# Gate weights of the first columns loaded in quarters, and the table load placed behind the second root

## The chip, the cores and the metric

The kernel runs on one core of a Trainium2 chip. The core has five engines that run side by side, each with its own list of instructions, executed in order: TensorE (PE in the profile; its weight loads are shown as PEld), VectorE (DVE), ScalarE (ACT), GpSimd (POOL) and the sync engine (SP), which issues DMA transfers. The metric is the device time of one execution in microseconds. Eight executions of the kernel before took 178.55 to 178.87 us, with a median of 178.8 us.

## The reference

The input x is a sequence of 2048 rows of 512 values (bf16). Its rows are normalized, and the result goes into two branches whose outputs are added to x:

```python
xn = _layernorm(x, axis=-1)
# A: a global filter in the frequency domain
X = rfft2(xn);  y_A = irfft2(X * (w_r + 1j * w_i), s=(S, D))
# B: a gated feed-forward block
g = einsum("bsd,df->bsf", xn, w_gate)      # 512 -> 1792
u = einsum("bsd,df->bsf", xn, w_up)        # 512 -> 1792
h = gelu_tanh(g) * u
y_B = einsum("bsf,fd->bsd", h, w_down)     # 1792 -> 512
return x + y_A + y_B
```

Layernorm here is `(x - mean) / sqrt(var + 1e-5)`. The change concerns the very beginning of the feed-forward branch: the first rows of x, the first columns of `w_gate` and the first products g and u.

## The kernel before

The 2048 rows are cut into 16 chunks of 128 rows (chunk c holds the rows 16p + c, one per partition p). Per chunk, VectorE takes mean and variance (`bn_stats`, L339, and `bn_aggr`, L342), the reciprocal root of the variance is formed, the rows are normalized to `xn`, and `xn` is transposed to `xnT`, so that the 512 inputs, as four blocks of 128, lie along the partitions. These four blocks (index e) are the contraction blocks of the gate and up products.

The feed-forward branch is a list of units (`todo`, L548 to L551). A unit computes g for some chunks and some blocks of 128 output columns into PSUM, u likewise, then gelu of g on ScalarE (L507) and the product with u on VectorE (L512), which gives a piece of `hT`. The first four units handle one chunk each: units 0 and 1 chunk 0, columns 0 to 511 and 512 to 1023; units 2 and 3 the same for chunk 1. Their sums are split over the contraction: before, each in two halves, blocks 0 and 1, then blocks 2 and 3 (`mm_part`, L502, 8 matmuls of 128x128x128 per half and unit). So TensorE can begin with half of the weights present. The units after these take two or four chunks at a time and come from L494. The down product (L833) and the inverse transform (L837) end the kernel.

The spectral branch runs between these units: folds on VectorE, small matmuls with cosine and sine tables, a twist with the filter weights, and exchanges through DMA.

What sets the order of the work: each engine's instructions are put in order by a planner written out in the kernel (`Plan`). Every operation has an engine, an estimated occupation and latency, its predecessors, a key (the lower, the sooner among those that could start) and possibly an earliest time `t_min`; counted resources stand for buffers (tags "G" and "U" for the sums of g and u, two buffers each; for units 0 to 3, "G" holds g and u of units 0 and 1, "U" those of units 2 and 3). The planner's times decide only the order; on the chip each instruction waits for the semaphores of what it needs.

All loads at the start are issued by the sync engine in program order (L281 to L306): x chunks 0 and 1, an index table, the gate weights of columns 0 to 1023 in two transfers of two contraction blocks (512 KB each), x chunks 2 and 3, the up weights of these columns likewise, x chunks 4 to 7 in two transfers, the remaining columns of both weights (768 KB each), x chunks 8 to 11 in two transfers, then tables, more of x, and the filter weights. The built program has eight completion semaphores for these transfers and uses them in turn: a transfer waits, before it is issued, for the completion of the one eight places before it.

`first_two` (L374) writes out chunks 0 and 1. Their root is `Sqrt` on ScalarE (L394) followed by a reciprocal on VectorE. Chunk 0 is normalized in two halves and transposed by TensorE (L351); chunk 1's transposes (`t`, 0 and 1) stand among the gate matmuls of units 0 and 1, after their first half (`between`, L532, with the keys of L422 and L423). VectorE copies the first half of chunk 1's transposes to `xnT`, ScalarE the second (`copyt1`). `Sqrt` and gelu need different activation tables, so ScalarE has to load the gelu table once after the last `Sqrt`; before, the planner has an entry for it, `table`, which issues no instruction (L412), and the load stands directly in front of the first gelu. TensorE is kept busy by 37 matmuls on zeros from the start (L320), and five more after chunk 0's transposes (L324).

Of the kernel before, what the change touches and what calls it, by code (L numbers as in the profile page):

```python
# [15 lines left out]
AF = mybir.ActivationFunctionType  # L16

S = 2048
# [3 lines left out]
NE = 4  # L22
# [179 lines left out]
def kernel(  # L202
# [80 lines left out]
    idx_t = pc.tile([P, 3], I32, name="idx_t")  # L283
    nc.sync.dma_start(out=idx_t[:], in_=nc.inline_tensor(idx_np, name="spec_rows").ap())  # L284
    for T in (Wg_sb, Wu_sb):
        for e in range(0, NE, 2):
            load_w(T, 0, 1024, e=slice(e, e + 2))
        if T is Wg_sb:
            load_x(2, 2)
    load_x(4, 2)  # L290
    load_x(6, 2)
    load_w(Wg_sb, 1024, DF)
    load_w(Wu_sb, 1024, DF)
    load_x(8, 2)
    load_x(10, 2)
    for c in range(0, NC, 8):
        nc.sync.dma_start(out=RF_t[:, c:c + 8], in_=rf_d.rearrange("p (c k) -> p c k", c=NC)[:, c:c + 8])
    load_x(12, 2)
# [8 lines left out]

    LAND = {0: 2.7, 1: 3.4, 2: 7.2, 3: 7.2}
    LAND.update({c: 11.5 if c < 8 else 17.5 if c < 12 else 20.5 for c in range(4, NC)})
    WG_LAND = [6.6] * 8 + [13.2] * 6  # L310
    WU_LAND = [9.9] * 8 + [15.2] * 6
    RF_LAND = 19.0

# [60 lines left out]
    def first_two():  # L374
        o = {}

        def v(k, fn, occ, deps=(), lat=None, t_min=0.0):
            o[k] = add("DVE", occ, fn, [o[d] for d in deps], key=-2000 + len(o), lat=lat, t_min=t_min,
                       after=o.get("last"))
            o["last"] = o[k]  # L380

        def T(c, h):
            o["T", c, h] = add("PE", 0.12, lambda: f_T(c, 2 * h, 2), [o["xn", c, h]], key=-2000 + 2 * c + h,
                               lat=0.36, acq=("S",))

        def xn_(c, h):
            v(("xn", c, h), lambda: f_norm_v(c, 256 * h, 256), 0.27, [("recip", c)], lat=0.4)

        def stats(c):
            v(("stats", c), lambda: f_stats(c), 0.6, t_min=LAND[c], lat=0.7)  # L390

        def mean(c):
            v(("mean", c), lambda: f_mean(c), 0.17, [("stats", c)])
            o["root", c] = add("ACT", 0.31, lambda: A.activation(  # L394
                out=rstd[:, c:c + 1], in_=mv[:, c, 1:2], func=AF.Sqrt, bias=eps_t[:], scale=1.0),
                [o["mean", c]], key=-2000 + c)

        def recip(c):
            v(("recip", c), lambda: V.reciprocal(out=rstd[:, c:c + 1], in_=rstd[:, c:c + 1]), 0.15, [("root", c)])

        stats(0)
        mean(0)
        stats(1)

        recip(0)
        xn_(0, 0)
        mean(1)
        xn_(0, 1)
        T(0, 0)
        T(0, 1)  # L410
        add("PE", 0.28, spin_on, [o["T", 0, 1]], key=-1500, lat=0.28, after=o["T", 0, 1])
        table = add("ACT", 1.3, lambda: None, [o["root", 1]], key=-1500, lat=1.3)  # L412
        v("copy0", lambda: f_Tc(0, 0, 2), 0.25, [("T", 0, 0)], lat=0.4)
        o["copy0"].rel = ("S",)
        xT_op[0, 0] = o["copy0"]
        recip(1)
        v("copy1", lambda: f_Tc(0, 2, 2), 0.25, [("T", 0, 1)], lat=0.4)
        o["copy1"].rel = ("S",)
        xT_op[0] = o["copy1"]
        xn_op[0] = o["xn", 0, 1]  # L420
        v("xn1", lambda: f_norm_v(1, 0, D), 0.33, [("recip", 1)], lat=0.45)
        o["t", 0] = add("PE", 0.12, lambda: f_T(1, 0, 2), [o["xn1"]], key=1000.13, lat=0.3, acq=("S",))  # L422
        o["t", 1] = add("PE", 0.12, lambda: f_T(1, 2, 2), [o["xn1"]], key=1000.14, lat=0.3, acq=("S",),  # L423
                        after=o["t", 0])
        between.update(o)
        v("copyt0", lambda: f_Tc(1, 0, 2), 0.25, [("t", 0)], lat=0.4)
        o["copyt1"] = add("ACT", 0.4, lambda: f_Tc(1, 2, 2, A.copy), [o["t", 1], table], key=-1400)
        o["copyt0"].rel = o["copyt1"].rel = ("S",)
        xT_op[1, 0] = o["copyt0"]
        xT_op[1] = o["copyt1"]  # L430
        xn_op[1] = o["xn1"]
# [42 lines left out]
    def unit(k, c0, n, f0, m=1):  # L474
# [19 lines left out]
                    T_.matmul(b[name][:, f], lhsT=W_[:, e, (f0 + f) * P:(f0 + f + 1) * P], rhs=rhs[:, e, :],  # L494
                              start=(e == 0), stop=(e == NE - 1))

        def mm_part(name, tag, W_, e0):
            if e0 == 0:
                b[name] = ps.tile([P, m, w], F32, name=name, tag=tag, bufs=2)
            for e in (e0, e0 + 1):  # L500
                for f in range(m):
                    T_.matmul(b[name][:, f], lhsT=W_[:, e, (f0 + f) * P:(f0 + f + 1) * P], rhs=rhs[:, e, :],  # L502
                              start=(e + f == 0), stop=(e == NE - 1), skip_group_check=True)
# [18 lines left out]

        gt, ut = "G", "U"
        if k < 4:
            def parts(name, tag, W_, key, t):
                o = None
                for e in (0, 2):
                    o = add("PE", occ / 2, lambda e=e: mm_part(name, tag, W_, e), [o] if o else [], lat=occ / 2 + 0.3,
                            key=key + 0.1 * e, acq=() if o else (tag,), t_min=t[e // 2])
                    o.deps.append(xT_op[c0, 0] if e == 0 else xT_op[c0])  # L530
                    if k == 1 and W_ is Wg_sb:
                        between["t", 0].deps.append(o) if e == 0 else o.deps.append(between["t", 1])  # L532
                return o

            gt = ut = "GU"[k // 2]
            g = parts("g_ps", gt, Wg_sb, 1000 + 0.1 * (k % 2) + 0.4 * (k // 2), (5.3, WG_LAND[0]))
            u = parts("u_ps", ut, Wu_sb, 1001 + 0.1 * (k % 2) + 0.4 * (k // 2), (8.6, WU_LAND[0]))
        else:
            g = split("g_ps", "G", Wg_sb, 1000 + k, WG_LAND, m)
            u = split("u_ps", "U", Wu_sb, 1000.5 + k, WU_LAND, m)  # L540
# [356 lines left out]
```

## Time and profile before

| | |
|---|---|
| median of 8 executions | 178.8 us (178.55 to 178.87) |
| profiled execution | 178.65 us, of which the span on the core is 177.0 us |
| TensorE busy | 171.7 us, 97% of the span |
| VectorE busy | 115.4 us, 65% |
| ScalarE busy | 96.4 us, 54% |
| GpSimd busy | 16.7 us, 9% |
| DMA | 19.35 MB, mean 109 GB/s; 344 to 390 GB/s from 4.4 to 22 us |
| gate and up sums of the first four units (L502) | 64 + 64 matmuls, from 6.10 to 14.5 us |
| gelu table load | 1.28 us, at 7.82 us |

The span runs from the first to the last instruction on the core; the profiled execution's time is 1.65 us longer than its span. Times in timelines are microseconds from the start of the span. A busy time counts the modelled ends of pipelined matmuls, so a busy TensorE is not one at its peak. The chain of work is followed back from the last instruction, at each step to what released it. In answers on waits a releaser is inferred from semaphores: the last to come is named. In the windows, each engine's entry is its busy time in the window with the number of instructions, then come the clock granted to TensorE, the busy share of the DMA engines, and GB/s.

### The profile page before, as it was taken

The numbers are of one execution on the slowest core, as the hardware profiler recorded it, in microseconds if no ns is written. First come the engines' busy times: TensorE is split into PE (matmuls) and PEld (weight loads), VectorE is DVE, ScalarE is ACT, GpSimd is POOL, SyncE is SP. The second block draws the span as 40 slices with busy tenths as digits, with TensorE's granted clock in tenths as the row PEclk, the third lists the DMA queues.
The fourth block names the chain that finished last, engine by engine and source line by source line (L and its number), as shares of the span: only waits on it lengthen the run. The fifth ranks groups of instructions, "written<-read, shape, count | busy, mean of one in ns | idle before, by whom it ended". The sixth has DMA issues, their size and how long they took to land.

```text
span 177.0 us, 3177 instructions
## 1 busy us (share of the span) xinstructions
PE 171.7 (97%) x1158; PEld 97.1 (55%) x1176; DVE 115.4 (65%) x255; ACT 96.4 (54%) x171; POOL 16.7 (9%) x38
## 2 busy tenths in 40 slices
PE   7999999999999999999999999999999999999993
PEld 7899845455545544555555454555445445444463
DVE  3568999988334499969899799843516325345333
ACT  4362489997734998889999973544112111211200
POOL 1020330407750000000000000000000000000000
DMA  4999999364609602111112312010122222221212
GB/s 100 347 390 381 344 195 150 61 82 94 225 20 313 224 0 59 44 34 44 38 26 61 94 56 59 17 46 0 59 90 89 79 74 66 82 88 60 63 59 59
DMA packets 20848, 19.35 MB, mean 109 GB/s; under 512 B 8481, under 2 KB 17953, under 8 KB 20833
## 3 DMA queue, kind: packets, MB, share of 16 engines
q1 hardware_dynamic: 20416, 17.84, 36.4%
q0 software_dynamic: 416, 1.32, 2.5%
q8 instruction: 9, 0.15, 0.3%
q14 instruction: 7, 0.05, 0.1%
HBM read 13.38 MB, written 2.10 MB: 87 GB/s over the span
## 4 chain that ended last, share of the span: by engine, by line
PE 91%; DMA 4%; SPq 2%; issue 1%; DVE 0%
PE y_ps L833 27%; PE g_ps L494 25%; PE u_ps L494 25%; DMA Wu_sb<-in_B_w_up_dram 4%; PE dp L651 2%; PE yp L784 2%; PE gp L754 2%; PE bp L593 2%; PE y_ps L837 2%; PE ep L660 2%; PE u_ps L502 2%; SPq L277 1%; SPq L273 1%; PE tp L351 0%; SPq L284 0%
## 5 line engine op out<-in xcount | busy, mean ns | idle before, releaser
L494 PE MATMUL g_ps<-xnT,Wg_sb 128*128 128x512 bf16 (+1 forms) x220 | 52.7, 364 | 0.3
L494 PE MATMUL u_ps<-xnT,Wu_sb 128*128 128x512 bf16 (+1 forms) x216 | 52.5, 363 | 0.3
L833 PE MATMUL y_ps<-Wd_sb,hT 128*128 128x512 bf16 (+2 forms) x246 | 50.8, 355 | 0.3
L512 DVE TENSOR_TENSOR hT<-u_ps,ge 128x512 bf16<-128x512 f32 x56 | 38.3, 687 | 17.3 <-PE u_ps L494 12.4
L507 ACT ACTIVATE ge<-g_ps 128x512 bf16<-128x512 f32 x56 | 33.2, 599 | 21.9 <-PE g_ps L494 19.1
L833 PEld LDWEIGHTS <-hT 128*128 128x128 bf16 x252 | 23.2, 98 | 22.2
L494 PEld LDWEIGHTS <-Wg_sb 128*128 128x128 bf16 x224 | 21.5, 98 | 20.9
L494 PEld LDWEIGHTS <-Wu_sb 128*128 128x128 bf16 x224 | 21.4, 98 | 20.2
L790 ACT CAST yf<-yp 128x512 bf16<-128x512 f32 x16 | 9.3, 586 | 39.4 <-PE yp L784 39.4
L840 DVE TENSOR_TENSOR y_sb<-y_ps,y_sb 128x512 bf16<-128x512 f32 (+2 forms) x18 | 11.1, 631 | 27.9 <-PE y_ps L837 27.9
L665 ACT CAST E<-ep 64x512 bf16<-64x512 f32 x32 | 18.5, 579 | 2.0 <-PE ep L660 1.6
L339 DVE BATCH_NORM_STATS2 stats<-x_t 128x6 f32<-128x512 bf16 x16 | 10.3, 672 | 2.7 <-DMA x_t<-in_A_x_dram 2.7
L456 ACT ACTIVATE xn<-x_t,nb,rstd 128x512 bf16<-128x512 bf16 x12 | 9.4, 807 | 0.6 <-POOL nb L370 0.4
L563 ACT CAST Gs<-gp 128x512 bf16<-128x512 f32 x16 | 8.7, 592 | 1.0 <-PE gp L754 1.0
L563 ACT CAST ds<-dp 128x512 bf16<-128x512 f32 x16 | 8.9, 597 | 0.0
L796 DVE TENSOR_TENSOR lv<-yf 128x512 bf16<-128x512 bf16 x16 | 6.1, 420 | 4.1 <-ACT yf L790 3.2
L563 ACT CAST Bs<-bp 128x512 bf16<-128x512 f32 x16 | 8.3, 600 | 0.5 <-PE bp L593 0.5
L784 PEld LDWEIGHTS <-Gs 128*128 128x128 bf16 x64 | 4.8, 98 | 3.5
L803 DVE TENSOR_TENSOR yt<-lv 128x512 bf16<-128x512 bf16 x16 | 6.1, 421 | 0.3
L837 PE MATMUL y_ps<-yt,RI_t 128*128 128x512 bf16 (+2 forms) x18 | 6.1, 355 | 0.0
L784 PE MATMUL yp<-CT,Gs 128*128 128x128 bf16 x64 | 6.0, 219 | 0.1
L697 DVE TENSOR_TENSOR m<-X,TW 128x1024 bf16<-128x1024 bf16 x8 | 5.5, 687 | 0.2
(67 smaller groups left out, 131.6 us busy)
## 6 DMA issues: line engine op xcount, KB each, us to landing
F<-F SPq DMA_DIRECT2D x32, 64.0 KB, 2.0
y_sb<-in_A_x_dram SPq DMA_DIRECT2D x16, 128.0 KB, 2.1
out_dram<-y_sb SPq DMA_DIRECT2D x15, 128.0 KB, 1.7
x_t<-in_A_x_dram SPq DMA_DIRECT2D x7, 256.0 KB, 8.7
Wd_sb<-in_B_w_down_dram SPq DMA_DIRECT2D x1, 1792.0 KB, 7.6
Wg_sb<-in_B_w_gate_dram SPq DMA_DIRECT2D x2, 512.0 KB, 4.3
Wu_sb<-in_B_w_up_dram SPq DMA_DIRECT2D x2, 512.0 KB, 6.8
Wg_sb<-in_B_w_gate_dram SPq DMA_DIRECT2D x1, 768.0 KB, 10.3
```

The lines of the kernel that those rows point to most:

```text
L339: V.bn_stats(out=st[:], in_=x_t[:, c, :])
L456: xn_op[c] = add("ACT", 0.72, lambda c=c: A.activation(out=xn[:, c, :], in_=x_t[:, c, :], func=AF.Identity, bias=nb[:, c:c + 1], scale=rst ...
L494: T_.matmul(b[name][:, f], lhsT=W_[:, e, (f0 + f) * P:(f0 + f + 1) * P], rhs=rhs[:, e, :], start=(e == 0), stop=(e == NE - 1))
L507: A.activation(out=b["ge"][:], in_=b["g_ps"][:], func=AF.Gelu_apprx_tanh)
L512: V.tensor_tensor(out=hT_of(sb, f0, m, o, w), in0=b["u_ps"][:], in1=b["ge"][:], op=ALU.mult)
L563: A.copy(out=o, in_=i)
L665: A.copy(out=b["E"][64 * h:64 * h + 64, r], in_=b["ep", h][64 * r:64 * r + 64])
L784: T_.matmul(t[:, q], lhsT=late["G"][:, q, c0 + j], rhs=IQ[q], start=(q == 0), stop=(q == 3), skip_group_check=True)
L790: A.copy(out=b["yf"][:, j], in_=b[j][:])
L833: T_.matmul(b[o][:], lhsT=hT_of(sb, f, 1, cl * P, P)[:, 0], rhs=Wd_sb[:, f, o:o + w], start=(f == 0), stop=False)
L837: T_.matmul(b[o][:], lhsT=late["RI"][:, c, :], rhs=late["yt"][:, c, o:o + w], start=False, stop=True)
L840: V.tensor_tensor(out=b["y"][:, o:o + w], in0=b[o][:], in1=b["y"][:, o:o + w], op=ALU.add)
```

## The change

Four things are edited.

1. The first 1024 columns of the gate weights come in four transfers of one contraction block (256 KB each) instead of two of two blocks. The up weights stay in two.
2. The gate sums of units 0 to 3 are advanced by quarters, one contraction block at a time (4 matmuls per unit), with keys of their own: blocks 0 and 1 of units 0 and 1, then chunk 1's transposes, then block 2 of units 0 and 1, block 3 of unit 0, blocks 0 and 1 of units 2 and 3, block 3 of unit 1, and blocks 2 and 3 of units 2 and 3. The up sums stay in halves in the same order as before. The number of matmuls is the same.
3. The planner's `table` entry now issues an instruction, a gelu of one column (`warm`), so that the table load stands directly behind the second root and ahead of `copyt1`.
4. x chunks 4 to 7 come in one transfer instead of two, and chunks 8 to 11 too. With edit 1 the number of transfers is as before, but the places of the semaphores shift: the transfers of the up weights are two places later.

Apart from this, every engine's order of instructions is as it was.

```diff
     for T in (Wg_sb, Wu_sb):
-        for e in range(0, NE, 2):
-            load_w(T, 0, 1024, e=slice(e, e + 2))
+        m = 1 if T is Wg_sb else 2
+        for e in range(0, NE, m):
+            load_w(T, 0, 1024, e=slice(e, e + m))
         if T is Wg_sb:
             load_x(2, 2)
-    load_x(4, 2)
-    load_x(6, 2)
+    load_x(4, 4)
     load_w(Wg_sb, 1024, DF)
     load_w(Wu_sb, 1024, DF)
-    load_x(8, 2)
-    load_x(10, 2)
+    load_x(8, 4)
...
-    WG_LAND = [6.6] * 8 + [13.2] * 6
+    WG_LAND = [7.3] * 8 + [13.2] * 6
...
-        table = add("ACT", 1.3, lambda: None, [o["root", 1]], key=-1500, lat=1.3)
+        table = add("ACT", 1.3, lambda: A.activation(out=warm[:], in_=eps_t[:], func=AF.Gelu_apprx_tanh), [o["root", 1]], key=-1500, lat=1.3)
...
-        o["t", 0] = add("PE", 0.12, lambda: f_T(1, 0, 2), [o["xn1"]], key=1000.13, lat=0.3, acq=("S",))
-        o["t", 1] = add("PE", 0.12, lambda: f_T(1, 2, 2), [o["xn1"]], key=1000.14, lat=0.3, acq=("S",),
+        o["t", 0] = add("PE", 0.12, lambda: f_T(1, 0, 2), [o["xn1"]], key=1000.04, lat=0.3, acq=("S",))
+        o["t", 1] = add("PE", 0.12, lambda: f_T(1, 2, 2), [o["xn1"]], key=1000.05, lat=0.3, acq=("S",),
                         after=o["t", 0])
...
-        def mm_part(name, tag, W_, e0):
+        def mm_part(name, tag, W_, e0, ne):
             if e0 == 0:
                 b[name] = ps.tile([P, m, w], F32, name=name, tag=tag, bufs=2)
-            for e in (e0, e0 + 1):
+            for e in range(e0, e0 + ne):
...
-            def parts(name, tag, W_, key, t):
-                o = None
-                for e in (0, 2):
-                    o = add("PE", occ / 2, lambda e=e: mm_part(name, tag, W_, e), [o] if o else [], lat=occ / 2 + 0.3,
-                            key=key + 0.1 * e, acq=() if o else (tag,), t_min=t[e // 2])
-                    o.deps.append(xT_op[c0, 0] if e == 0 else xT_op[c0])
+            def parts(name, tag, W_, keys, t):
+                o, ne = None, NE // len(keys)
+                for i, key in enumerate(keys):
+                    e = i * ne
+                    o = add("PE", occ / len(keys), lambda e=e: mm_part(name, tag, W_, e, ne), [o] if o else [],
+                            lat=occ / len(keys) + 0.3, key=key + 0.01 * (k % 2), acq=() if o else (tag,), t_min=t[i])
+                    o.deps.append(xT_op[c0, 0] if e < 2 else xT_op[c0])
                     if k == 1 and W_ is Wg_sb:
-                        between["t", 0].deps.append(o) if e == 0 else o.deps.append(between["t", 1])
+                        if i == 1:
+                            between["t", 0].deps.append(o)
+                        elif i == 2:
+                            o.deps.append(between["t", 1])
                 return o
...
-            g = parts("g_ps", gt, Wg_sb, 1000 + 0.1 * (k % 2) + 0.4 * (k // 2), (5.3, WG_LAND[0]))
-            u = parts("u_ps", ut, Wu_sb, 1001 + 0.1 * (k % 2) + 0.4 * (k // 2), (8.6, WU_LAND[0]))
+            g = parts("g_ps", gt, Wg_sb, ((1000, 1000.02, 1000.06, 1000.12), (1000.08, 1000.1, 1000.14, 1000.16))[k // 2],
+                      (5.35, 6.0, 6.65, 7.3))
+            u = parts("u_ps", ut, Wu_sb, (1001 + 0.4 * (k // 2), 1001.2 + 0.4 * (k // 2)), (8.9, 10.3))
```

## The prediction

> **What bounds the kernel now.** I read the profile from the outside in: first the chain of work that ended last, to see which engine sets the end; then who waited for whom on TensorE, to see where that engine is not fed; then the timelines of the first 16 us, since all of the change lies there; then the DMA traffic in half-microsecond windows, to see whether that traffic can go any faster. The shares of the chain by engine:
>
> ```profile
> PE 91%; DMA 4%; SPq 2%; issue 1%; DVE 0%
> ```
>
> TensorE carries 91% of the chain, and one transfer nearly all of the rest. The waits of the matmul unit and of its weight loads, over the whole span (engine, line, waited for: us in total, times, longest):
>
> ```profile
> PE g_ps L502 <- DMA Wg_sb<-in_B_w_gate_dram: 0.3, 1, 0.3
> PE u_ps L502 <- DMA Wu_sb<-in_B_w_up_dram: 0.2, 1, 0.2
> PEld L502 <- DMA Wg_sb<-in_B_w_gate_dram: 0.6, 2, 0.4
> PEld L502 <- DMA Wu_sb<-in_B_w_up_dram: 0.4, 1, 0.4
> ```
>
> After the warm-up TensorE waits only for gate and up weights. Which of these waits counts? The chain in order of time (start, us, what):
>
> ```profile
> 4.15 7.19 DMA Wu_sb<-in_B_w_up_dram
> 11.34 0.05 issue
> 11.39 0.62 PE u_ps L502 x8
> ```
>
> The last wait of TensorE ends when the second half of the first up weights lands, at 11.34 us. From 11.39 on TensorE runs without a wait to the end; the gate weights are not on this chain. TensorE before that point (start, us, what, count, idle before):
>
> ```profile
> 6.10 1.07 PE L502 MATMUL g_ps<-xnT,Wg_sb 128*128 128x128 bf16 x16 [0.26 <-DMA Wg_sb<-in_B_w_gate_dram]
> 7.00 0.39 PE L351 MATMUL tp<-ident_t,xn 128*128 128x128 bf16 x4
> 7.40 2.85 PE L502 MATMUL g_ps<-xnT,Wg_sb 128*128 128x128 bf16 x48
> 10.09 1.06 PE L502 MATMUL u_ps<-xnT,Wu_sb 128*128 128x128 bf16 x16
> 11.39 0.62 PE L502 MATMUL u_ps<-xnT,Wu_sb 128*128 128x128 bf16 x8 [0.25 <-DMA Wu_sb<-in_B_w_up_dram]
> ```
>
> The 48 gate matmuls take 2.69 us from start to start of the next row, 0.056 us each; the 16 up matmuls end near 10.99 and 0.4 us passes empty. ScalarE in the same time:
>
> ```profile
> 5.03 0.29 ACT L394 ACTIVATE rstd<-mv,eps_t 128x1 f32<-128x1 f32 x1 [0.82 <-DVE mv L342]
> 7.43 0.37 ACT L354 COPY xnT<-tp 128x256 bf16<-128x256 bf16 x1 [2.11 <-PE tp L351]
> 7.82 1.28 ACT L507 ACT_TABLE_LOAD   x1
> 9.11 2.06 ACT L507 ACTIVATE ge<-g_ps 128x512 bf16<-128x512 f32 x4
> ```
>
> ScalarE has 2.11 us empty ahead of the copy, and loads the table after it. Last the traffic; the two final figures of each row are the busy share of the DMA engines and GB/s:
>
> ```profile
> 3.50:4.00 0.50, 0.50 (x7) 0.50 (x6) 0.47 (x3) 0.08 (x1) 0.00 (x0) 1.00 0.14 45
> 4.00:4.50 0.50, 0.50 (x8) 0.50 (x6) 0.50 (x2) 0.21 (x1) 0.00 (x0) 1.00 0.90 315
> 5.50:6.00 0.50, 0.34 (x7) 0.17 (x4) 0.50 (x4) 0.00 (x0) 0.00 (x0) 1.00 1.06 414
> 7.50:8.00 0.50, 0.50 (x11) 0.50 (x11) 0.11 (x1) 0.48 (x2) 0.00 (x0) 1.00 0.89 225
> 10.50:11.00 0.50, 0.50 (x12) 0.47 (x9) 0.00 (x0) 0.50 (x2) 0.47 (x1) 1.00 1.05 402
> ```
>
> From 4.0 us on the engines are full. So the up weights land when the bytes ahead of them have gone by, not when they are issued: issued at 3.67 and 4.15, they land at 9.97 (6.3 us later in the list of issues) and 11.34. The gate halves, issued at 2.18 and 2.65, land at 6.08 and 7.35 (3.9 and 4.7 us), and chunks 2 and 3 of x at 8.26 (3.16 plus 5.1).
>
> **What the Trainium skill says.** "DMA: Bandwidth & Descriptors", Queues, rings and completion order: on each DMA engine the descriptors of one queue are consumed in ring order. The landings above, all in order of issue, agree. The same page, Anatomy of one DMA: a transfer has a fixed part of about 2 us, mostly the acknowledgement of its last bytes rather than time in which nothing moves. The 128 KB of x chunk 0 take 2.1 us here, and full windows across the boundary of the two gate halves (414 GB/s at 5.5 to 6.0) show no hole. "ScalarE: Activation LUTs", What ACT_TABLE_LOAD costs: a load is about 1283 ns; the trace has 1.28 us. "TensorE: Matmul & The Clock Gate", Part 1: the array returns to half clock after an idle window of about 3.4 us; the 37 warm-up matmuls, at 3.86 / 37 = 0.104 us each by their weight loads, and the gate matmuls, at 0.056, agree with two clocks; the longest hole here is 0.4 us.
>
> **The change part by part.**
>
> *Gate weights in four transfers.* Same bytes, same packets of one 2 KB row per partition. A half takes 7.35 - 6.08 = 1.27 us to pass, so a quarter 0.64: landings at about 5.44, 6.08, 6.72 and 7.35. Issue: sync spends 0.47 us per transfer, so the four start at 2.18, 2.65, 3.12 and 3.59, then x chunks 2 and 3 at 4.06 (was 3.16), the up halves at about 4.55 and 5.0 (were 3.67 and 4.15). The up halves' bytes pass at about 8 to 9.5 and 9.5 to 11, so 0.9 us of later issue uses up a small part of several microseconds of queue. In the built program each sync transfer waits for the completion of the one eight places before it; with two more gate transfers the up halves now wait for x chunks 0 and 1, which land at 2.9 and 3.4: no cost. Bound: nothing to 0.1 us at the up landing if the acknowledgements of two more transfers delay the ring; I take 0. If the queue ran dry it would be the whole 0.9.
>
> *Gate units by quarters.* TensorE runs the same 64 gate matmuls and the same four transposes of chunk 1, in the same place after 16 matmuls. The first copy of xnT ends at 5.70, so block 0 runs 5.75 to 6.2 (8 x 0.056 = 0.45), block 1 6.2 to 6.65, the transposes to about 7.0, block 2 to 7.45 and the other 40 matmuls (40 x 0.056 = 2.24) to about 9.7, against 10.09 before: 0.4 us sooner. Next in line is the first up half at 9.97, so of the 0.4 us at most 0.1 reaches the up matmuls; they run 10.0 to 10.9 and then wait for 11.34. What remains of the gain becomes a longer wait at that same point: 0.
>
> *Table behind the second root.* The root ends at 5.32, the load at 6.60, the small gelu (as the first small root, 0.29) at 6.9. Behind it stands the copy of chunk 1's second half, whose transposes end near 7.0 to 7.1: not delayed; with no cover left it would cost 0.1 to 0.3 us at the gate matmuls of chunk 1, which have the 0.4 us. The four gelus then run from about 7.9 instead of 9.11 and end near 10.6 instead of 11.17. Their consumer, hT, waits for up sums on VectorE until 12.12, so nothing comes of it: 0.
>
> *x in pieces of four chunks.* Two issues fewer, behind the up weights. Chunks 4 to 7 then count as landed with the last of them, before too near 13.9 (issued near 5.2, some 8.7 us), used at 15.56: 0. Chunks 8 to 11 land with chunk 11, near 19.5 (issued at 9.73, 9.8 us later), and VectorE wants chunk 8 at 19.41: some 0.1 to 0.2 us of delay there. Behind it stand products that free up-sum buffers; I measured the time between such a product's end and the up matmuls that reuse its buffer, and from the fifth unit pair on it is 0.7 us or more, 1.1 around this place: 0. Its price without that slack is the same 0.1 to 0.2. The later transfers are issued sooner, into a full queue.
>
> Sum: 0 - 0 - 0 + 0 = 0, with -0.1 to +0.1 from the up landing. The profiled execution has a span of 177.0 us and 1.65 us around it, 178.65, which is 0.15 below the median of 178.8. I predict 178.7. The eight runs lie 0.32 us apart, 0.18%; 0.2%, 0.36 us, is about what can be told from no change.
>
> **The rivals.**
>
> *The stream starts sooner (faster).* At 3.5 to 4.0 the DMA engines are nearly idle (45 GB/s) although gate weights have been issued at 2.18. If a transfer of half the descriptors starts sooner, or the slow start in the window of 315 GB/s shrinks, all that follows moves up by as much as 0.5 us, the last up half from 11.34 to 10.84, and TensorE is ready for it (gate end 9.7, first up part then by 10.5). That gives 178.2 to 178.4. For it: that hole. Against it: the down weights, one transfer of 14 rows per partition, begin to move about 1.0 us after their issue, as x chunk 0 does, so the size does not set the start; and the hole may be slow first reads of that matrix, which stay. It counts as faster from 0.36 us on.
>
> *Each boundary costs (slower).* At 7.0 to 8.0, where x and the up weights follow each other, the rate falls to 262 and 225 GB/s; against some 390 that is about 0.37 us lost. If that is the price of a boundary of transfers, two more gate boundaries cost 0.74 us ahead of the up half, which lands at about 12.1: 179.5. It decides from 0.18 us per boundary on. Against it: the boundary between the gate halves shows no dip.
>
> *Late issue or a cold array (slower).* If TensorE's second hole of about 0.3 us at 9.7 lets its clock drop, a microsecond or more is lost: some 180. A hole far under an idle window speaks against it.
>
> *The gate wait was the bound after all.* If some of the 0.4 us lived on, 178.4; the chain denies it, and it is counted with the faster ones.
>
> **How the numbers follow.** No visible change 0.62 (its own range 178.4 to 179.1); faster, by the sooner stream or a surviving part of the gate gain, 0.23; slower by boundaries 0.11, by late issue or clock 0.04. The range of 178.2 to 179.3 holds the first whole, two thirds of the faster cases and the small boundary prices, about 0.8. Slower is then 0.15.
>
> **What would show it.** Right: the first gate matmuls near 5.75; gate matmuls over by about 9.7; table load at 5.3; a longer wait for up weights, still released near 11.34; the rest of TensorE shifted by under 0.1. A release below 11.0 is the sooner stream, above 11.7 the boundaries, with dips at 5 to 7 us. The forecast is wrong if the last up half moves, or if TensorE waits anywhere after it.

## The result, and the profile after

The changed kernel is slower: 180.29 us (median of 20 runs), against 178.86 us for the kernel before (57 runs beside them). The ratio is 1.0077, with a 95% interval of 1.0068 to 1.0087. Two later comparisons of the same two kernels (h1 and h5 below) gave 0.74 and 1.28 us instead of 1.43. A run more than 1.5% above the fastest of its kernel counts as slow, and the ratios, and the times of e1 and e4, leave such runs out. The forecast was 178.7 us, with 179.3 as the upper end of its range.

The profiled execution of the changed kernel took 179.62 us, with a span of 177.9 us (before: 178.65 and 177.0). It is one of the quicker executions of this kernel, so the trace shows 0.97 us of the 1.4.

The chain of work that ended last has the same shares by engine as before, TensorE 91% and DMA 4%. In order of time (start, us, what) it still runs through the second half of the first up weights:

```profile
5.02 7.15 DMA Wu_sb<-in_B_w_up_dram
12.17 0.05 issue
12.22 0.62 PE u_ps L501 x8
```

So the chain has the same form, and its release moved from 11.34 to 12.17 us: 0.83 of the 0.97 us. The transfer is issued 0.87 us later (5.02 against 4.15) and takes as long as before from there (7.15 against 7.19). The waits of the matmul unit in the whole span (engine, line, waited for: us in total, times, longest):

```profile
PE u_ps L501 <- DMA Wu_sb<-in_B_w_up_dram: 0.3, 1, 0.3
PE g_ps L501 <- DMA Wg_sb<-in_B_w_gate_dram: 0.2, 1, 0.2
```

and of its weight loads:

```profile
PEld L501 <- DMA Wu_sb<-in_B_w_up_dram: 0.7, 2, 0.4
PEld L501 <- DMA Wg_sb<-in_B_w_gate_dram: 0.4, 1, 0.4
```

The second wait for up weights is new: the first up half too is now late. TensorE in order of time (start, us, operation, count, idle before):

```profile
6.07 1.46 PE L501 MATMUL g_ps<-xnT,Wg_sb 128*128 128x128 bf16 x16
7.37 0.39 PE L350 MATMUL tp<-ident_t,xn 128*128 128x128 bf16 x4
7.59 0.61 PE L501 MATMUL g_ps<-xnT,Wg_sb 128*128 128x128 bf16 x8
8.42 2.41 PE L501 MATMUL g_ps<-xnT,Wg_sb 128*128 128x128 bf16 x40 [0.22 <-DMA Wg_sb<-in_B_w_gate_dram]
10.88 1.07 PE L501 MATMUL u_ps<-xnT,Wu_sb 128*128 128x128 bf16 x16
12.22 0.62 PE L501 MATMUL u_ps<-xnT,Wu_sb 128*128 128x128 bf16 x8 [0.27 <-DMA Wu_sb<-in_B_w_up_dram]
```

The gate matmuls were to end sooner and end later. 40 of them wait for the fourth quarter until 8.42; the second half of before had landed at 7.35. The first up matmuls start at 10.88 instead of 10.09, and then comes the old wait. (The first 16 gate matmuls are slow: their weight loads take 1.39 us, before 0.90. In this execution the loads follow each other at 0.107 us until 6.9 us, then at 0.056. It costs nothing here, since the later quarters had not landed.) ScalarE does what was forecast:

```profile
5.41 1.28 ACT L411 ACT_TABLE_LOAD   x1
7.79 0.37 ACT L353 COPY xnT<-tp 128x256 bf16<-128x256 bf16 x1 [0.89 <-PE tp L350]
8.86 0.60 ACT L506 ACTIVATE ge<-g_ps 128x512 bf16<-128x512 f32 x1 [0.69 <-PE g_ps L501]
```

The table is loaded at 5.41, ahead of the copy, and the first gelu then waits for gate sums, not for the table. Last the traffic in half-microsecond windows (the two final figures are the busy share of the DMA engines and GB/s):

```profile
3.50:4.00 0.50, 0.50 (x7) 0.50 (x6) 0.47 (x3) 0.01 (x1) 0.00 (x0) 1.00 0.49 160
5.00:5.50 0.50, 0.50 (x6) 0.28 (x5) 0.33 (x3) 0.39 (x2) 0.00 (x0) 1.00 0.78 213
5.50:6.00 0.50, 0.50 (x7) 0.50 (x6) 0.50 (x4) 0.50 (x1) 0.00 (x0) 1.00 0.77 283
7.50:8.00 0.50, 0.50 (x13) 0.50 (x10) 0.29 (x1) 0.21 (x1) 0.00 (x0) 1.00 0.85 275
10.50:11.00 0.50, 0.45 (x8) 0.28 (x6) 0.50 (x3) 0.43 (x2) 0.00 (x0) 1.00 1.06 418
```

Two things happen. The stream starts a little sooner (160 GB/s at 3.5 to 4.0 instead of 45), and then, while the quarters pass, it runs at 213 and 283 GB/s from 5.0 to 6.0; the halves had 414 at 5.5 to 6.0. From 9.5 us on it is as quick as before. From TensorE's last wait to the first gate matmul of the later units, at 15.49 instead of 14.53, another 0.13 us is lost, around the transposes of chunks 2 and 3. After that nothing is lost or won: from there to the last matmul it is 159.65 us in both kernels.

So the time goes into the landing of the up weights. The experiments ask which edit is at fault, and by which of three ways:

- **L**: x chunks 2 and 3 and the up weights are *issued* some 0.9 us later, behind two more transfers.
- **S**: the gate transfers are *shorter*, and there are more of them ahead of the up weights.
- **W**: the up weights are now the ninth and tenth transfers, so they use a completion *semaphore* a second time and wait for it.

The table gives the landings in the profiled executions of the kernels that issue their first gate weights at 2.17 us; what each kernel is follows below. The trace has, for each transfer, the times at which its 16 DMA engines finished. "The Trainium skill", page "DMA: Bandwidth & Descriptors", section "Why a DMA increments its semaphore by 16 and not by 1", says that these engines finish independently and that only the full count means that all data has landed. So the last engine counts, and the median engine shows how the stream as a whole stands. The KB (of 1000 bytes) are worked out from the rates of the windows 3 to 5 and 5 to 8 us. The last column is the difference of the medians to the kernel before in the same comparison. Each landing is that of one execution.

| kernel | gate in | last up half issued | median engine | last engine | last minus median | KB, 3 to 8 us | time, us |
|---|---|---|---|---|---|---|---|
| before | halves | 4.15 | 10.99 | 11.34 | 0.35 | 1433 | |
| e3, x in fours | halves | 4.15 | 10.84 | 11.21 | 0.37 | 1462 | +0.13 |
| e2, change with halves | halves | 4.15 | 10.79 | 11.64 | 0.85 | 1444 | +0.20 |
| e6, semaphores shifted | halves | 4.16 | 10.94 | 11.41 | 0.47 | 1448 | +0.36 |
| e5b, late issue | halves | 5.10 | 10.71 | 12.32 | 1.61 | 1496 | +0.77 |
| e5c, later still | halves | 6.39 | 11.44 | 12.32 | 0.88 | 1326 | +0.94 |
| e4, two short transfers | halves | 5.23 | 10.89 | 15.44 | 4.55 | 1393 | +1.72 |
| h2, change with halves, late | halves | 5.14 | 11.04 | 12.23 | 1.19 | 1463 | +0.78 |
| h6, the same again | halves | 4.85 | 11.10 | 11.99 | 0.89 | 1407 | +0.60 |
| changed kernel | quarters | 5.02 | 11.44 | 12.17 | 0.73 | 1301 | +1.43 |
| h1, the same again | quarters | 5.03 | 11.48 | 12.19 | 0.71 | 1292 | +0.74 |
| h5, the same again | quarters | 5.03 | 11.26 | 12.63 | 1.37 | 1266 | +1.28 |
| e1, split alone | quarters | 5.03 | 11.45 | 12.70 | 1.25 | 1313 | +1.90 |
| h4, change, other up order | quarters | 5.03 | 11.25 | 12.78 | 1.53 | 1351 | +0.46 |

### The profile page after: what moved, and what is told of

Same layout as the page of the kernel before. It is cut to its first block, busy times and chain, and to the rows that moved or that the text cites. A ratio compares the mean times of both kernels' runs of the same rounds, so it can differ in the third digit from the quotient of the medians.

```text
span 177.9 us, 3179 instructions
## 1 busy us (share of the span) xinstructions
PE 172.6 (97%) x1158; PEld 97.8 (55%) x1176; DVE 115.6 (65%) x255; ACT 96.8 (54%) x172; POOL 16.7 (9%) x38
## 4 chain that ended last, share of the span: by engine, by line
PE 91%; DMA 4%; SPq 2%; issue 1%; DVE 0%
PE y_ps L837 27%; PE g_ps L493 25%; PE u_ps L493 25%; DMA Wu_sb<-in_B_w_up_dram 4%; PE yp L788 2%; PE dp L655 2%; PE bp L597 2%; PE gp L758 2%; PE y_ps L841 2%; PE ep L664 2%; PE u_ps L501 2%; SPq L277 1%; SPq L273 1%; PE tp L350 0%; SPq L284 0%
## 5 line engine op out<-in xcount | busy, mean ns | idle before, releaser
L506 ACT ACTIVATE ge<-g_ps 128x512 bf16<-128x512 f32 x56 | 33.4, 599 | 23.3 <-PE g_ps L493 19.2
L844 DVE TENSOR_TENSOR y_sb<-y_ps,y_sb 128x512 bf16<-128x512 f32 (+2 forms) x18 | 11.1, 631 | 27.9 <-PE y_ps L841 27.9
```

Of the source, the lines that this page charges most:

```text
L506: A.activation(out=b["ge"][:], in_=b["g_ps"][:], func=AF.Gelu_apprx_tanh)
L844: V.tensor_tensor(out=b["y"][:, o:o + w], in0=b[o][:], in1=b["y"][:, o:o + w], op=ALU.add)
```

## Experiments: which edit

**The split alone** (e1), on the kernel before:

```diff
-        for e in range(0, NE, 2):
-            load_w(T, 0, 1024, e=slice(e, e + 2))
+        m = 1 if T is Wg_sb else 2
+        for e in range(0, NE, m):
+            load_w(T, 0, 1024, e=slice(e, e + m))
```

> Kernel before with one edit: the first gate weights in four transfers; TensorE's halves, the table and x stay as they were. Theory S (the split itself slows the stream: each short transfer costs time at its start or end): the last up half lands near 12.2 us instead of 11.34 and the time is 0.8 to 1.4 us above before. Theory L (not the split but the up weights' later issue, 0.9 us): the same, since the issue is as late here. Theory R (the rest of the change, x in fours, the early table load or the quarters on TensorE): the up half lands near 11.4 and the time is within 0.2 us of before.

180.71 us (five runs), ratio 1.0102 (1.0068 to 1.0135). The split alone is at least as slow as the whole change. In its profile, 0.4 us of the loss lies behind the last matmul and its last transfer, not at the weights: from the first gate matmul of the later units to the end of the span it takes 162.85 us, the kernel before 162.43.

**The change with the gate back in halves** (e2):

```diff
-        m = 1 if T is Wg_sb else 2
+        m = 2
```

> Changed kernel with the gate weights back in two transfers; quarters on TensorE, early table and x in fours stay. Theories S and L: the up half lands near 11.4, time within 0.2 us of before (178.6 to 179.0). Theory R: 0.8 to 1.4 us above before.

179.02 us, ratio 1.0011 (1.0002 to 1.0019). Gate sums by quarters on TensorE, the early table and x in fours are all in this kernel, and together they cost at most 0.2%. Its chain:

```profile
4.15 7.49 DMA Wu_sb<-in_B_w_up_dram
11.64 0.05 issue
```

**x in fours alone** (e3), on the kernel before:

```diff
-    load_x(4, 2)
-    load_x(6, 2)
+    load_x(4, 4)
...
-    load_x(8, 2)
-    load_x(10, 2)
+    load_x(8, 4)
```

> Kernel before with only x chunks 4 to 7 and 8 to 11 in one transfer each. Theories S and L: within 0.2 us of before. Theory R, if x in fours is what slows: 0.8 us or more above before.

178.95 us, ratio 1.0006 (0.9997 to 1.0015): no cost that can be told from none.

**Two more transfers without the split** (e4): the gate stays in halves, and two copies of the index table (1.5 KB each) stand between the gate and x chunks 2 and 3.

```diff
         if T is Wg_sb:
+            for j in range(2):
+                tiny = pc.tile([P, 3], I32, name=f"tiny{j}")
+                nc.sync.dma_start(out=tiny[:], in_=nc.inline_tensor(idx_np, name=f"tiny_rows{j}").ap())
             load_x(2, 2)
```

> Kernel before with two more transfers of 1.5 KB (a second and third copy of the index table, not used by anything) between the gate weights and x chunks 2 and 3. Gate transfers stay whole; x and the up weights are issued 0.9 us later, as in the changed kernel, and there are two more boundaries between transfers. Theory L (late issue): the up half lands 0.5 us or more later, time 0.5 to 1.4 us above before. Theory S as a price of every boundary: the same 0.8 us. Theory S as a matter of short gate transfers alone: the up half near 11.4 to 11.5, time within 0.3 us of before.

180.53 us (three runs, 180.42 to 182.63; a fourth took 184.81), ratio 1.0131 (1.0058 to 1.0203), more than any of the three ways had foretold. Shorter gate transfers are not needed for a loss. The profiled execution was the longest, 184.81 us, and what it shows holds for it alone. Its median engine has the last up half at 10.89, as before, but one engine is 4.55 us behind it, at 15.44. TensorE waits (start, us, operation, count, idle before):

```profile
12.52 1.07 PE L505 MATMUL u_ps<-xnT,Wu_sb 128*128 128x128 bf16 x16 [1.59 <-DMA Wu_sb<-in_B_w_up_dram]
15.49 0.84 PE L505 MATMUL u_ps<-xnT,Wu_sb 128*128 128x128 bf16 x8 [1.90 <-DMA Wu_sb<-in_B_w_up_dram]
16.98 3.44 PE L505 MATMUL u_ps<-xnT,Wu_sb 128*128 128x128 bf16 x40
```

These four leave the loads ahead of the up weights as the cause, and all three ways open: each slower kernel has its up weights later in issue, behind more transfers, and on semaphores used before.

## Experiments: issue time, shortness or semaphore

**Late issue alone** (e5b), on the kernel before: the same transfers in the same order on the same semaphores. A one-element copy on GpSimd, behind the landing of the index table, writes into x chunk 2, so that the load of chunks 2 and 3, and in SP's order all that follows, must wait for it. The loads are held to the written order (`pin`, not shown for each).

```diff
         if T is Wg_sb:
-            load_x(2, 2)
+            nc.gpsimd.tensor_copy(out=x_t[0:1, 2, 0:1], in_=idx_t[0:1, 0:1]); pin(load_x(2, 2))
```

> The kernel before with the same transfers in the same order and the same semaphores, but x chunks 2 and 3 (and with them, in SP's order, the up weights) wait for a one-element copy on GpSimd behind the landing of the index table (3.8 us), so they are issued about 0.9 us later, as in the changed kernel (near 4.1, 4.6 and 5.1). Theory L (the later issue of these transfers is what makes the up half land late): 180.0 to 180.8, last up half near 12.2. Theory S (short transfers and their boundaries ahead of the up weights cost the time, whenever they are issued): 178.8, last up half 11.3. Theory W (the up weights use completion semaphores a second time and wait for them): 178.8.

179.66 us, ratio 1.0029 (0.9997 to 1.0062); taken alone, this interval doesn't quite exclude no loss, the next run's and those of h2 and h6 do. The time lies below the 180.0 to 180.8 that L had foretold. The issues came at 4.24, 4.62 and 5.10. TensorE:

```profile
7.53 2.85 PE L502 MATMUL g_ps<-xnT,Wg_sb 128*128 128x128 bf16 x48 [0.19 <-DMA Wg_sb<-in_B_w_gate_dram]
11.04 1.07 PE L502 MATMUL u_ps<-xnT,Wu_sb 128*128 128x128 bf16 x16 [0.66 <-DMA Wu_sb<-in_B_w_up_dram]
12.36 0.62 PE L502 MATMUL u_ps<-xnT,Wu_sb 128*128 128x128 bf16 x8 [0.25 <-DMA Wu_sb<-in_B_w_up_dram]
```

The gate is on time and the up weights are late, the last half at 12.32, as L said. But the median engine is not late at all, 10.71. One engine falls behind with x chunks 2 and 3: it ends them at 9.63, where the median has 7.75 and the last but one 8.47. The last landing stays 1.8 and 1.6 us behind the median in both up halves; the trace gives the 16 times without the engines' names, so that it is the same engine is inferred.

**Later still** (e5c): seven copies instead of one. The up weights are issued at 5.92 and 6.39, 2.2 us later than before.

```diff
-            nc.gpsimd.tensor_copy(out=x_t[0:1, 2, 0:1], in_=idx_t[0:1, 0:1]); pin(load_x(2, 2))
+            [nc.gpsimd.tensor_copy(out=x_t[0:1, 2, 0:1], in_=idx_t[0:1, 0:1]) for _ in range(7)]; pin(load_x(2, 2))
```

> As the run with late issue alone, but behind seven copies instead of one, so that x chunks 2 and 3 are issued near 5.4 and the up weights near 5.8 and 6.3, some 2.1 us later than before, and still 1.6 us before the gate weights are through. Theory L, if the loss grows with the delay (0.77 us for 1.0): 180.2 to 181. If any lateness costs the same: 179.5 to 179.9. If the 0.77 was not from lateness: 178.9 to 179.2.

179.74 us, ratio 1.0065 (1.0041 to 1.0089); five runs. The loss does not grow with the delay. Here all engines are late (median 11.44, last 12.32), with 154 GB/s from 7 to 8 us.

**Semaphores used again, at unchanged issue times** (e6): the two small transfers are issued by ScalarE at the very start.

```diff
+    for j in range(2):
+        tiny = pc.tile([P, 3], I32, name=f"tiny{j}")
+        pin(nc.scalar.dma_start(out=tiny[:], in_=nc.inline_tensor(idx_np, name=f"tiny_rows{j}").ap()))
     pin(nc.scalar.activation(out=warm[:], in_=eps_t[:], func=AF.Sqrt, bias=eps_t[:], scale=1.0))
```

> The kernel before with two transfers of 1.5 KB more, issued by ScalarE at the very start, ahead of its first table load. SP issues everything at the same times as before, but the two up transfers are now the ninth and tenth, so they wait for a semaphore as in the changed kernel. Theory W: 180.0 to 181.0. Theory L: 178.8. Theory S: 178.8, since the short transfers are over before the gate weights begin; if their mere number counted, 180 to 181.

179.25 us, ratio 1.0005 (0.9980 to 1.0031). The up weights are issued at 3.68 and 4.16, wait for a semaphore each, and land at 11.41. In the profile the later units start at 14.63, where before has 14.53; of the 0.48 us by which its span is longer, 0.37 lie behind the last matmul, as in e1. W falls: the semaphores cost nothing that this shows, and cannot be the 1.4 us.

**Issue 0.47 us sooner** (e7): the index table is loaded behind the up weights instead of ahead of the gate.

```diff
-    nc.sync.dma_start(out=idx_t[:], in_=nc.inline_tensor(idx_np, name="spec_rows").ap())
     for T in (Wg_sb, Wu_sb):
...
             load_x(2, 2)
+    nc.sync.dma_start(out=idx_t[:], in_=nc.inline_tensor(idx_np, name="spec_rows").ap())
```

> The kernel before with the index table (1.5 KB) loaded behind the up weights instead of ahead of the gate weights; all else as before. Gate weights, x chunks 2 and 3 and the up weights are issued 0.47 us sooner and have one short transfer less ahead of them. Theory L: up to 0.5 us faster, 178.3 to 178.5, last up half 10.9 to 11.1. Theory S: 178.4 to 178.7. Theory W: 178.8, since the up weights have first-use semaphores in both.

178.62 us, ratio 0.9979 (0.9961 to 0.9996), within what S had foretold and less than L's gain. The last up half lands at 10.91; TensorE no longer waits for it, and the second gate half, at 7.42, takes its place on the chain.

**The split with that sooner issue** (e8): the diff of e7 and that of e1 together. The up weights are issued at 4.07 and 4.55.

> The gate weights in four transfers as in the changed kernel, and the index table behind the up weights: gate units still advance by halves. x chunks 2 and 3 and the up weights are issued 0.45 us later than before, half as much as with the split alone, and only the last up transfer uses a semaphore a second time. Theory L: 179.2 to 179.8, between before (178.8) and the split alone (180.8). Theory S: 180.0 to 180.8, as with the split alone. Theory W: 179.5 to 180.8, by the last up transfer.

179.72 us, ratio 1.0039 (1.0016 to 1.0061): between before and the split alone, as L said. Against e7, the same kernel with halves and with the up weights issued 0.87 us sooner, it is 1.1 us. The median engine is at 10.68, as in e7 (10.64), the last at 12.58. By 8.0 us it has moved 1451 KB, e7 1560.

**The whole change, issued early** (f1): x chunk 1 is issued by ScalarE and the index table goes behind the up weights, so that x chunks 2 and 3 and the up weights are issued at 3.13, 3.60 and 4.08, as before the change.

```diff
+    pin(load_x(1, 1, nc.scalar))
     pin(nc.scalar.activation(out=warm[:], in_=eps_t[:], func=AF.Sqrt, bias=eps_t[:], scale=1.0))
     pin(load_x(0, 1))
-    pin(load_x(1, 1))
```

> The changed kernel whole (four gate transfers, gate units by quarters, early table), but x chunk 1 is issued by ScalarE at the start and the index table behind the up weights, which takes two issues out of SP's list ahead of the gate weights: the gate quarters are issued from 1.24 on, x chunks 2 and 3 near 3.1, the up weights near 3.6 and 4.1, as in the kernel before. Theory L (later issue of x chunks 2 and 3 and of the up weights is the whole cause): 178.6 to 179.0. Theory S (shorter transfers and more of them ahead of the up weights cost the time, whenever issued): 179.3 to 180.0. Both in equal parts: 179.2.

178.89 us against 178.80, ratio 1.0027 (1.0003 to 1.0051): most of the 1.4 us is gone, with all four quarters in place.

**The kernel before, issued early** (f2), with the same two moves (the diffs of f1 and e7) and halves:

> The kernel before with the same two moves (x chunk 1 issued by ScalarE, index table behind the up weights) and the gate weights in halves: everything from the gate weights on is issued 0.94 us sooner. Theory L: 178.1 to 178.5. Theory S: 178.5 to 178.8 (one short transfer less ahead). In both the second gate half, near 7.0, then becomes what TensorE waits for.

178.90 us, ratio 1.0026 (1.0008 to 1.0043). A miss: nothing was gained. The up weights do land sooner (11.04), but the gate weights now run beside x chunks 0 and 1, which land at 4.03 and 4.21 instead of 2.95 and 3.41. The chain begins there:

```profile
4.05 0.70 DVE stats L339
4.76 0.02 issue
4.78 0.18 DVE mv L342
```

So f1 and f2 are equal in time, but under another bound, and f1 is weaker evidence against S than its time says. In bytes the split still shows: 1516 KB by 8.0 us in f1, 1620 in f2.

**Two short transfers, issued early** (f3): the diff of f2 and that of e4.

> The kernel of f2 with two transfers of 1.5 KB between the gate weights and x chunks 2 and 3: x chunks 2 and 3 and the up weights are issued about when the kernel before issues them (3.2, 3.7, 4.2), but two short transfers lie in front of them. Theory L: 178.7 to 179.0. Theory S: 180 to 181.5, as when the two were added without the earlier issue.

179.12 us, ratio 1.0043 (1.0015 to 1.0071). Where e4 lost 1.7 us, the same two transfers here cost 0.2 against f2 by the medians. The up weights, issued at 3.87 and 4.35, land with their last engine at 10.75, 0.41 behind the median. Nine of the 20 runs took 180.5 us or more, the profiled one too, so that the mean is 0.6 us above that of f2; the reason seen in the profile lies on TensorE and is told below.

## Experiments on the changed kernel itself

**The changed kernel again, beside its version with halves and late issue.** h1 and h5 are the changed kernel; h2 and h6 are e2 with the GpSimd copy of e5b (both diffs above). Each pair ran on one chip.

> The changed kernel once more, as the measure for the two runs beside it, and for a second look at its landings: 180.3, with the last up half near 12.2 and, on the median DMA engine, near 11.4.

> The changed kernel with the gate weights in halves, while x chunks 2 and 3 and the up weights are held back behind a one-element copy on GpSimd, so that they are issued as late as in the changed kernel (4.2, 4.6 and 5.1). With halves and no delay this kernel took 179.0, the changed kernel 180.3. Theory L alone: 180.3. Theory S alone: 179.0. Both, as late issue and the split did on the kernel before: 179.6 to 179.8, with the median engine at 10.7 to 11.0 for the last up half and single engines up to 1.5 us behind it.

> The changed kernel once more. Its cost has been 1.4 us in the first comparison and 0.7 us in the last one: here 0.7 to 1.5 us above before.

> The changed kernel with gate halves, x chunks 2 and 3 and the up weights held back as before. Theory L alone (late issue is the whole cost): the same as the changed kernel beside it, within 0.3 us. Theory S and L together: 0.7 to 0.9 us above before, and the changed kernel beside it 0.4 us or more slower than this, where it costs 1.2 us or more.

| | quarters | halves, late issue | before |
|---|---|---|---|
| first pair | 179.48, ratio 1.0044 (1.0029 to 1.0060) | 179.52, ratio 1.0039 (1.0026 to 1.0053) | 178.74 |
| second pair | 180.09, ratio 1.0059 (1.0040 to 1.0079) | 179.41, ratio 1.0032 (1.0012 to 1.0052) | 178.81 |

The first pair was expected at 180.3 for the changed kernel and took 0.8 us less. With late issue and no split at all the kernel is 0.32 to 0.39% slower than before, 0.6 to 0.7 us; 0.2 us of this may belong to the other edits, which e2 has without late issue. The split adds nothing in the first pair and 0.27%, 0.5 us, in the second, where the intervals overlap. TensorE of h2:

```profile
7.55 2.85 PE L501 MATMUL g_ps<-xnT,Wg_sb 128*128 128x128 bf16 x48
10.97 1.07 PE L501 MATMUL u_ps<-xnT,Wu_sb 128*128 128x128 bf16 x16 [0.57 <-DMA Wu_sb<-in_B_w_up_dram]
12.28 0.62 PE L501 MATMUL u_ps<-xnT,Wu_sb 128*128 128x128 bf16 x8 [0.24 <-DMA Wu_sb<-in_B_w_up_dram]
```

and of h5:

```profile
8.40 2.41 PE L501 MATMUL g_ps<-xnT,Wg_sb 128*128 128x128 bf16 x40 [0.36 <-DMA Wg_sb<-in_B_w_gate_dram]
11.33 1.07 PE L501 MATMUL u_ps<-xnT,Wu_sb 128*128 128x128 bf16 x16 [0.52 <-DMA Wu_sb<-in_B_w_up_dram]
12.68 0.62 PE L501 MATMUL u_ps<-xnT,Wu_sb 128*128 128x128 bf16 x8 [0.28 <-DMA Wu_sb<-in_B_w_up_dram]
```

Both wait twice for up weights. With quarters the gate is late as well.

The table above shows the two parts side by side. Among kernels with issue as before, the last engine is 0.35 to 0.85 us behind the median; with late issue it is 0.7 to 1.6 behind, with halves and quarters alike (4.55 in the one execution of e4). With quarters the median engine is at 11.25 to 11.48, with halves at 10.71 to 11.10, issued up to 1 us late or not; 2.2 us late, in e5c, it is at 11.44 too. So in these profiles late issue shows in one to three engines that fall behind, and the split in the whole stream: 1266 to 1351 KB by 8.0 us against 1407 to 1496 for halves without e4 and e5c, on average some 145 KB, or 0.4 us at 390 GB/s. With everything issued sooner the bytes at 8.0 us still differ by about 105 KB (e8 and e7, f1 and f2), but the median engine by 0.04 and 0.15 us only.

**Other work ahead of the wait** (h4): the changed kernel, with the first up halves of units 2 and 3 put ahead of the second up half of unit 0 in the planner's finished list. The loads are untouched.

```diff
-        for op in plan.order():
+        seq = plan.order()
+        early = [between["u_ps", 2, 0], between["u_ps", 3, 0]]
+        for op in early:
+            seq.remove(op)
+        at = seq.index(between["u_ps", 0, 1])
+        for op in seq[:at] + early + seq[at:]:
```

(`between[name, k, i]` keeps the planner's entries of `parts`.)

> The changed kernel with one difference on TensorE: the first up halves of units 2 and 3 (16 matmuls, 0.9 us) are put ahead of the second up half of unit 0, so that TensorE has work until 12.5 to 12.7 and the last up half may land until then. Loads are untouched. If the wait for the last up half is the only way by which the change costs time, 179.1 to 179.6, and no wait for it is left; what remains above 178.8 is the later start of the first up half. If something later in the kernel costs the time too, 180 or more.

179.20 us, ratio 1.0025 (1.0013 to 1.0037); the changed kernel beside it took 179.48 us. TensorE in the profiled execution:

```profile
11.48 2.41 PE L501 MATMUL u_ps<-xnT,Wu_sb 128*128 128x128 bf16 x40 [0.96 <-DMA Wu_sb<-in_B_w_up_dram]
13.72 0.61 PE L350 MATMUL tp<-ident_t,xn 128*128 128x128 bf16 x8
```

The last up half landed at 12.78 and nobody waited for it. What is left is the wait for the first up half, 0.96 us here. Nothing later in the kernel costs time: from the first gate matmul of the later units to the end it is 162.4 us, as before.

**A version that beats both** (g1): the change with halves (e2), the index table behind the up weights (e7) and the up order of h4.

> A version to beat both: gate weights in halves, index table behind the up weights (all issues 0.47 us sooner than before), early table load and x chunks 4 to 11 in fours as in the changed kernel, and the up order of the run beside it. TensorE should have no wait from the landing of the second gate half (7.3 to 7.5) on: 178.2 to 178.5. If the second gate half or the first up half lands late instead: 178.8.

178.42 us (21 runs), ratio 0.9980 (0.9973 to 0.9988). TensorE waits for no weights but the second gate half, on the chain, which lands at 7.05:

```profile
7.10 2.85 PE L501 MATMUL g_ps<-xnT,Wg_sb 128*128 128x128 bf16 x48
9.79 2.40 PE L501 MATMUL u_ps<-xnT,Wu_sb 128*128 128x128 bf16 x40
```

## Why the prediction was wrong

**What bounds the kernel** was read rightly: the landing of the last up half released TensorE in both kernels, and 0.83 of the 0.97 us in the trace is the shift of that landing.

**The step that failed** is "0.9 us of later issue uses up a small part of several microseconds of queue", with "nothing to 0.1 us" as its bound. It took a transfer that is queued for 6 us as safe from 0.9 us of delay, and kept "the whole 0.9" for a queue that runs dry. In its place the runs show a loss of 0.77 us for that delay alone (e5b, by the medians); h2 and h6, with the other edits, are 0.78 and 0.60 above before, where e2, the same without the delay, is 0.20 above. The reading behind it, that the up weights land when the bytes ahead of them have gone by, holds for the median engine (10.71 in e5b, with late issue) and not for the last one, and the matmuls wait for the last. The prediction looked at landings and rates, which hide the spread over 16 engines; the 0.35 us between median and last engine before was no fixed property, it is up to 0.85 us with the same issue (e2). Nor were the engines "full" from 4.0 us on: the prediction's own rows have 262 and 225 GB/s at 7.0 to 8.0, just where x chunks 2 and 3 pass, the transfer with which an engine falls behind in e5b.

**A second step in the same sum** was too small: "a quarter 0.64". The four quarters landed at 4.95, 6.24, 7.11 and 8.38, so they passed in 1.29, 0.87 and 1.27 us after the first. The Trainium skill, "DMA: Bandwidth & Descriptors", section "Rules for kernel authors", asks for 1 MiB or more in a transfer where bandwidth counts; 256 KB against 512 KB agrees in direction, and the price here is about 0.4 us of stream by the bytes above.

**Gate by quarters.** The first gate matmuls started at 6.07, 5.66 and 5.67 in three profiles (forecast 5.75; in the first, the five zero matmuls ahead of them ran at 0.107 us each), so the first step was right. "Over by about 9.7" was wrong by a microsecond, since the fourth quarter came a microsecond late, and thus the 0.4 us that was to disappear into the wait never arose.

**Table, x in fours, semaphores**: the table load at 5.41 (forecast 5.3) with no delay of the copy; e3 and e2 show nothing above 0.2%, e6 nothing for the semaphores. These zeros were right.

**The rivals.** "Each boundary costs" gave 179.5 us and a landing near 12.1, and its signs (dips at 5 to 7 us, a release above 11.7) came true. It had 0.11. Its landing was near the truth for a reason that covers a part only: without one more boundary, late issue alone brings the landing to 12.0 to 12.3. Late issue stood in the forecast only beside a cold array, at 0.04 for both. "The stream starts sooner" came true at its start, with 160 GB/s for 45 and the first quarter at 4.95 where 5.44 was forecast, and the gain was gone with the second quarter (6.24, forecast 6.08).

**What stays open.** Why an engine falls behind when its next descriptors are issued 2.8 instead of 3.9 us ahead of use (x chunks 2 and 3, issued at 4.24 in e5b and 3.16 before, with the gate weights over at 7.1 on the median engine). From 3 to 10 us every profile has 15 to 34 single 2 KB packets of 0.3 us or more, up to 1.6, where the usual one takes 0.084, and from 10 to 20 us at most two; whether the descriptors or the memory make them slow, and whether engines run dry between transfers, no run here tells. Nor is the split's own share of the time settled: 0 in one pair, 0.5 to 0.7 us in the other, and in the first comparison what 1.43 us leaves beside the 0.77 of e5b, which was measured in another. All landings come from one profile per kernel and session.

## What to carry to other kernels

A transfer with microseconds of queue ahead of it is not safe from being issued later: count the issues of the sync engine (0.47 us each) ahead of the transfer that ends the last wait, and move what is not needed early, such as a small table, behind it. Splitting a transfer to start its consumer sooner can be paid by everything issued after it; ask what the consumer's next wait is first. And compare the last of the 16 engines with the median one: a landing that is late on one engine alone won't show in the rate.

## What the runs showed of the hardware

- **The last of the 16 engines can lag for the rest of the stream, and not by late issue alone.** In e5b the last engine is 0.4 us behind the median with the gate weights, 1.9 us with the 256 KB of x chunks 2 and 3, and still 1.6 us after 1 MB of up weights; in e4 it ends 4.55 us behind. But in the kernel before, x chunks 6 and 7, issued at 5.26, land at 13.93, 1.24 us after the last but one engine, and such a lag stays to 18.1 us. There the trace has one packet of 16 KB on the instruction queue, from 11.71 us, that takes 1.06 us; that it sits on the lagging engine is inferred. Every profile has such a packet, at 11.1 to 13.5 us. In e5b, where it starts at 11.46, the lag is older.
- **TensorE can fall to half rate without a long hole.** In e4's profiled execution two holes of 1.59 and 1.90 us, with 0.9 us of matmuls between them, come ahead of a change of rate at 15.7 us, in the middle of 8 matmuls: from there the weight loads follow each other at 0.107 us instead of 0.056, until 19.2 us, and the granted clock is 0.50 from 16 to 19 us. 40 matmuls take 3.27 us instead of 2.23. The Trainium skill, "TensorE: Matmul & The Clock Gate", Part 1, names an idle window of about 3.4 us; here neither hole is that long, and in the 3.4 us ahead of the change the weight loads are busy for 1.15 us.
- **The full rate comes at a different time in each execution.** In the changed kernel's profile the weight loads change from 0.107 to 0.056 us at 6.9 us, in f2's at 4.1, and in f3's only at 10.15. There the gate begins at half rate, after a hole of 0.77 us:

```profile
5.94 0.72 PE L354 MATMUL tp<-ident_t,xn 128*128 128x128 bf16 x4 [0.77 <-DVE xn L348]
6.99 1.91 PE L505 MATMUL g_ps<-xnT,Wg_sb 128*128 128x128 bf16 x16
```

The 16 matmuls take 1.91 us where f2, at full rate since 4.1 us, has 1.06 after a longer hole (1.35 us). The later units start 1.73 us later than in f2 (16.32 and 14.59), which fits the two groups of f3's runs, 179.0 to 179.1 and 180.5 to 181.1.

- **x chunk 0 lands later when more is issued beside it.** In f2, with the gate weights issued at 1.24 instead of 2.17 and x chunk 1 by ScalarE at the same time as chunk 0, x chunk 0 (128 KB), issued as before, landed a microsecond later (4.03 instead of 2.95). Which of the two moves does it was not separated.
